# Attention and a gated layer on one core: TensorE's written-out order re-solved, first-block products allowed both single PSUM banks, VectorE named first for two kinds of low parts

## The chip, the cores and the metric

The kernel runs on one core of a Trainium2 chip. The metric is the device time of one execution in microseconds (us). TensorE (PE) multiplies matrices into PSUM banks; VectorE (DVE), ScalarE (ACT) and GpSimd (POOL) work element by element; SyncE (SP) and POOL issue most DMAs. Each engine works its own list of instructions in order and waits on semaphores for the others.

## The reference, cut to what matters

```python
q_bits = (np.einsum('bhsd,dk->bhsk', q, proj) > 0)      # 6 hash bits a row; same for k
mask = q_bucket[:, :, :, None] == k_bucket[:, :, None, :]
scores = np.where(mask, scale * np.matmul(q, k.transpose(0, 1, 3, 2)), -1e9)
attn = softmax(scores)                                   # max taken off, 1e-09 added to the sum
x = (attn @ v).transpose(0, 2, 1, 3).reshape(B * S, H * D)
out = (sigmoid(x @ w_gate) * (x @ w_val)) @ w_out
```

There are 4 batches of 8 heads, 768 rows and a head dimension of 64, so 3072 tokens of width 512; the inner width of the gated layer is 1536. Inputs are float32. To keep their precision, operands are split into a high part in TensorE's float32 format and a low part (what is left), and three products high-low, low-high, high-high are added in PSUM.

## The kernel before, in words

**Attention stage (start to about 405 us).** Sixteen pairs of heads, each in two groups of 384 queries. Per group TensorE does six score tasks (tile `sc`, lines 1551 and 1557: one matmul pair for the hash bits, three for the split products), six transposes (`tp`, L1614) and six value products (`pv`, L1630). A score task fills a double PSUM bank; VectorE takes the minimum and copies it out (`e`, L1569), ScalarE takes the exponential (L1578), TensorE transposes, VectorE or ScalarE copies the transposed block back (`e`, L1620), and TensorE multiplies by the values. There are three double banks, so a score or transpose task waits until the bank of three tasks earlier has been read. Beside that run the preparation of the next pair (transposes `tk` and `tq`, raw copies `rawk` and `rawq`, low parts `kl` and `ql`, a hash product `h`) and the splitting of the gated layer's weights (lines 689 to 712 and 821 to 836), which is spread over VectorE, ScalarE and POOL.

**First block (about 405 to 445 us).** For each of the two groups of batch 0 (a unit) the products of the first two blocks of the inner width are done on their own, `moe_early`: `zg` and `zv` (gate and value, L896), the gated value `gf` (L913), its high and low parts `gh` and `gl` (lines 919 and 920), and the output products `zo` (L932). They wait for the end of the last attention task. A unit first needs its tokens in parts: `load_x` loads `xr`, POOL casts the high part `xh` (L867), and the low part `xl` (L870) may go to POOL or VectorE. Each of these products has one of the two single PSUM banks (tag `one`).

**Remaining products (to the end).** All other blocks go through a seven-product scheme for 2 by 2 blocks (`zB`, `zA`, `zD`, L1178) and output products `y` (L932), with weights streamed in by POOL's DMAs (`wsg`, `wsv`, L1728).

**What sets the order.** Every piece of work is a task with a key and one or more engines that may do it. TensorE follows the list `ORDER`, word for word. For the other engines a planner plays the tasks through with costs written in the code, takes at each free engine the ready task with the smallest key (key plus `SHIFT`, a number for each task), and so fixes each engine's list when the program is built. A task with several engines named stands in the queue of each of them, with 3 added to its key for each place further back; the planner asks the engines in the order PE, ACT, POOL, DVE, SP. Stock such as `one` (2) and `moe` (1) bounds in the planner how many tasks hold a bank at once; the waits of the running program come from the tiles alone.

Of the kernel before, what the change touches and what calls it, by code (L numbers as in the profile page):

```python
# [507 lines left out]
def lsh_attention_glu_kernel(ctx, tc, q, k, v, proj, w_gate, w_val, w_out, out):  # L508
    nc = tc.nc
# [375 lines left out]

    def product(key, u, n, j, x, prev, last, pace=None):

        z = {"bank": ["moe", "one"]}

        def part(c):  # L890
            if c == 0:
# [885 lines left out]
```

## Time and profile before

| what | value |
|---|---|
| runs of the kernel before | 965.33 us median of 3 (964.59 to 965.78) |
| profiled execution, its own time | 965.6 us |
| span of its trace | 963.8 us |
| granted TensorE clock | 0.999 |
| PE busy | 952.0 us (99%) |
| VectorE, ScalarE, POOL busy | 608.2, 548.2, 274.3 us |

Busy is the time in which an engine has at least one instruction at work. Matmuls are pipelined, so a busy PE may still have short waits inside. The time from the span to the execution's own time (1.8 us) lies outside the trace.

### The profile page before, as it was taken

To read this page: it belongs to the slowest core of one execution; us is meant where nothing else is said; L and a number is where in the kernel's file an instruction comes from. 1 tells how busy PE (TensorE), PEld (TensorE's weight loads), DVE (VectorE), ACT (ScalarE), POOL (GpSimd) and SP (SyncE) were. 2 spreads that over 40 slices of the span, in tenths; PEclk is the share of its full clock that TensorE was granted. 3 is DMA by queue.
4 is the path that set the end of the run, shared out by engine and by line. 5 is a ranking of instruction groups with operands and counts; after the bars stand their busy time and mean duration, and the time that the engine had idled before them with its cause. 6 is when DMAs were issued, how large, how long until landed. Compare 5 with 4: busy or idle time off the path is not lost.

```text
span 963.8 us, 20105 instructions
## 1 busy us (share of the span) xinstructions
PE 952.0 (99%) x8067; PEld 774.8 (80%) x8070; DVE 608.2 (63%) x1173; ACT 548.2 (57%) x993; POOL 274.3 (28%) x325
## 2 busy tenths in 40 slices
PE   9999999999999999999999999999999999999998
PEld 5666665666666567689999999999999999999997
DVE  7999898999899898676656743334633336333332
ACT  5988898898888889554334433324433235333322
POOL 4444655666765665630000000000000000000000
PEclk9999999999999999999999999999999999999999
DMA  7666888888897877489966774444744444644421
GB/s 186 175 194 189 224 252 241 244 249 238 263 268 213 233 228 228 171 315 411 370 237 230 280 262 175 153 153 154 271 170 158 170 177 173 222 154 153 154 78 66
DMA packets 116606, 204.37 MB, mean 212 GB/s; under 512 B 63456, under 2 KB 87968, under 8 KB 110624
## 3 DMA queue, kind: packets, MB, share of 16 engines
q1 hardware_dynamic: 107456, 118.08, 39.9%
q0 software_dynamic: 6688, 84.42, 23.7%
q8 instruction: 63, 1.03, 0.4%
q10 hardware_dynamic: 2368, 0.59, 0.3%
q14 instruction: 31, 0.25, 0.1%
HBM read 147.84 MB, written 43.42 MB: 198 GB/s over the span
## 4 chain that ended last, share of the span: by engine, by line
PE 92%; DVE 4%; DMA 2%; ACT 1%; issue 1%; SPq 0%; ACTq 0%; DVEq 0%
PE y L932 20%; PE pv L1630 12%; PE zBg L1178 10%; PE zBv L1178 10%; PE sc L1557 9%; PE tp L1614 7%; PE zDv L1178 5%; PE zDg L1178 5%; PE sc L1551 4%; PE zAg L1178 2%; PE zAv L1178 2%; PE h L1452 1%; DVE e L1569 1%; PE zg L896 1%; PE zv L896 1%; PE idle L642 1%
## 5 line engine op out<-in xcount | busy, mean ns | idle before, releaser
L1569 DVE TENSOR_SCALAR_CACHE_REDUCE e<-sc 128x768 f32<-128x768 f32 x192 | 177.1, 952 | 20.3 <-PE sc L1557 18.5
L1578 ACT ACTIVATE e<-e,st 128x768 f32<-128x768 f32 x192 | 178.9, 933 | 15.1 <-DVE e L1569 13.2
L932 PE MATMUL y<-wo,gh 128*128 128x512 f32 x480 | 151.0, 396 | 0.0
L1630 PE MATMUL pv<-e,vr 128*64 128x384 f32 x768 | 140.7, 496 | 0.0
L1620 ACT COPY e<-tp 128x768 f32<-128x768 f32 x144 | 112.2, 795 | 27.9 <-PE tp L1614 27.1
L1614 PEld LDWEIGHTS tp<-ident,e 64*128 64x128 f32 x2304 | 87.0, 138 | 45.7 <-issue 13.7
L1178 PE MATMUL zBg<-x,wsg 128*128 128x384 f32 x552 | 111.0, 335 | 0.0
L1178 PE MATMUL zBv<-x,wsv 128*128 128x384 f32 x552 | 110.7, 335 | 0.0
L1178 PEld LDWEIGHTS zBg<-x,wsg 128*128 128x128 f32 x552 | 98.2, 188 | 6.6 <-ACT t1g L1186 0.4
L1178 PEld LDWEIGHTS zBv<-x,wsv 128*128 128x128 f32 x552 | 98.3, 188 | 6.0
L932 PEld LDWEIGHTS y<-wo,gh 128*128 128x128 f32 x480 | 89.9, 187 | 15.2
L1614 PE MATMUL tp<-ident,e 64*128 64x64 f32 x2304 | 99.6, 226 | 1.8 <-DVE e L1569 0.9
L1271 ACT CAST gh<-zt 128x384 fp32r<-128x384 f32 x92 | 47.1, 514 | 95.1 <-DVE zt L1266 75.5
L932 PE MATMUL y<-wo,gl 128*128 128x512 f32 x240 | 93.2, 388 | 0.0
L1557 PE MATMUL sc<-kh,ql 64*128 64x384 f32 x192 | 89.8, 468 | 0.0
L1557 PE MATMUL sc<-kh,qsl 64*128 64x384 f32 x192 | 89.8, 468 | 0.0
L1630 PEld LDWEIGHTS pv<-e,vr 128*64 128x64 f32 x768 | 48.2, 136 | 51.3 <-issue 43.0
L1728 POOL DMA_DIRECT2D wsv<-kzv x23 | 12.2, 532 | 236.9 <-PE zDg L1178 224.6
L1728 POOL DMA_DIRECT2D wsg<-kzg x23 | 12.3, 536 | 227.4 <-PE zDv L1178 206.9
L1250 ACT ACTIVATE sig<-sig 128x384 f32<-128x384 f32 x69 | 36.2, 525 | 61.7 <-DVE sig L1193 61.6
L1274 DVE TENSOR_TENSOR gl<-zt,gh 128x384 fp32r<-128x384 f32 x92 | 51.0, 554 | 29.2 <-ACT gh L1271 29.2
L1551 PE MATMUL sc<-kq 64*128 64x384 bf16 x384 | 64.8, 328 | 2.3 <-ACT e L1620 1.1
(214 smaller groups left out, 1964.4 us busy)
## 6 DMA issues: line engine op xcount, KB each, us to landing
wsg<-kzg POOLq DMA_DIRECT2D x23, 1792.0 KB, 8.1
wsv<-kzv POOLq DMA_DIRECT2D x23, 1792.0 KB, 7.6
kzg<-wkg SPq DMA_DIRECT2D x12, 896.0 KB
kzv<-wkv SPq DMA_DIRECT2D x12, 896.0 KB
rawg<-in_moe_w_gate_dram SPq DMA_DIRECT2D x14, 512.0 KB
rawv<-in_moe_w_val_dram SPq DMA_DIRECT2D x14, 512.0 KB
vr<-in_v_dram SPq DMA_DIRECT2D x16, 384.0 KB
rb<-rd SPq DMA_DIRECT2D x64, 96.0 KB
```

Source lines behind the costliest of these rows:

```text
L932: nc.tensor.matmul(acc, a[:, slot, ts_], w, start=(first and i == 0), stop=(last and i == 2), skip_group_check=cols != slice(None),)
L1178: nc.tensor.matmul(acc, streams[n, jp][:, c, wa, a_], X[x_][:, xa, c], start=first and c == 0 and i == 0, stop=c == 1 and i == 2, skip_gro ...
L1250: lambda blk=blk: nc.scalar.activation(sig[:, blk], w["B"][:, :GN] if blk == 2 else sig[:, blk], AF.Sigmoid),
L1271: nc.scalar.copy(side["h"][:, blk], w["z", blk])
L1274: eng.tensor_sub(side["l"][:, blk], w["z", blk], f(side["h"][:, blk]))
L1551: nc.tensor.matmul(sc[:, j, :GN], kq[z["h"]][rows, 2 + 2 * g + h, t * P : (t + 1) * P], kq[z["h"]][rows, h], start=True, stop=False, tile_ ...
L1557: nc.tensor.matmul(sc[:, j, :GN], q_[rows, c], z["k" + x][rows, h * GN : (h + 1) * GN], start=False, stop=(m == 2), tile_position=(j * D, 0),)
L1569: nc.vector.tensor_scalar(sp(e), gz["sc", t, h][:, :, :GN], -MASKED * SCALE, None, op0=ALU.min, op1=ALU.min, accum_out=gz["st", t][:, h : ...
L1578: nc.scalar.activation(e, e, AF.Exp, bias=st[:, h : h + 1], scale=-1.0, accum_out=gz["su"][:, h * GT + t : h * GT + t + 1],)
L1614: nc.tensor.transpose(tp[:, r, at_ : at_ + D], gz["e", t, h][rows, c * P : (c + 1) * P], ident[rows, rows], tile_position=(r * D, 0),)
L1620: copy(gz["e"][:, :, c * P : (c + 1) * P].rearrange("p n (r d) -> p r n d", r=2), gz["tp", c][:, :, :GN].rearrange("p r (n d) -> p r n d", ...
L1630: nc.tensor.matmul(gz["pv"][rows, :GN], z["v"][:, h, c], gz["e"][:, h * GT : (h + 1) * GT, c * P : (c + 1) * P], start=(c == 0), stop=(c = ...
```

## The change

Three things. The stock `moe` is no longer taken by the first-block products whose key is at least 1e4, which is all of them here; they take only `one`. For the low parts `xl` and `gl` VectorE is now named first and POOL second. And `ORDER` and `SHIFT` are new throughout the attention stage and the first block. No computation is added or taken away.

```diff
@@ load_x
-                [("pool", 965, lambda c=c: low(c, nc.gpsimd)), ("dve", 470, lambda c=c: low(c, nc.vector))],
+                [("dve", 470, lambda c=c: low(c, nc.vector)), ("pool", 965, lambda c=c: low(c, nc.gpsimd))],
@@ product
-        z = {"bank": ["moe", "one"]}
+        z = {"bank": ["one"] if key >= 1e4 else ["moe", "one"]}
@@ gated
-            FIRST, [("pool", 965, lambda: low(nc.gpsimd)), ("dve", 470, lambda: low(nc.vector))],
+            FIRST, [("dve", 470, lambda: low(nc.vector)), ("pool", 965, lambda: low(nc.gpsimd))],
@@ moe_early
-        bank = ["y"] if ended else ["moe", "one"]
+        bank = ["y"] if ended else ["one"] if key >= 1e4 else ["moe", "one"]
@@ ORDER (first line of the attention stage that differs)
-    3, 4, 5, 6, 7, 8, 9, 10, 11, 12, 13, 14, 15, 39, 16, 17, 18, 42, 19, 20, 48, 21, 45, 51, 22, 23, 24, 25, 26, 53,
+    3, 4, 5, 6, 7, 8, 9, 10, 11, 12, 13, 14, 15, 39, 16, 17, 18, 42, 19, 20, 48, 21, 22, 45, 51, 23, 24, 25, 26, 27,
```

Three places of the engines' lists. In the names the first number is a buffer, the last one a running number; lines of the changed kernel are 22 higher.

The first is VectorE's list about a quarter of the way through the attention stage, where the tokens of the first unit (`xr_0`) are split. Before:

```order
L1569 TENSOR_SCALAR e_0_1_2237,st_0_1_2_2391<-sc_0_1_2_1_2382 128x768
L870 TENSOR_TENSOR xl_0_2409<-xr_0_2267,xh_0_2408 128x384
L707 SCALAR_TENSOR_TENSOR exv_0_2374<-rawv_0_2239,exv_0_2374 128x512
L870 TENSOR_TENSOR xl_0_2409<-xr_0_2267,xh_0_2408 128x384
L1637 TENSOR_TENSOR xs_3_1_2484<-pv_3_1_2255,rb_3_1_2151 128x384
L870 TENSOR_TENSOR xl_0_2409<-xr_0_2267,xh_0_2408 128x384
L1569 TENSOR_SCALAR e_1_0_2505,st_1_0_0_2504<-sc_1_0_0_0_2475 128x768
```

and with the change:

```order
L1591 TENSOR_SCALAR e_0_1_2277,st_0_1_2_2396<-sc_0_1_2_1_2387 128x768
L892 TENSOR_TENSOR xl_0_2413<-xr_0_2306,xh_0_2412 128x384
L724 SCALAR_TENSOR_TENSOR mfg_0_2383<-rawg_0_2235,mfg_0_2383 128x512
L1591 TENSOR_SCALAR e_1_0_2475,st_1_0_0_2474<-sc_1_0_0_0_2443 128x768
L1642 COPY e_0_0_2019<-tp_0_0_3_2456 128x2x6x64
```

Of the four low parts of this unit VectorE had three and now has one; POOL has the other three. The low parts `gl` stand on the same engines as before (three on POOL, one on VectorE).

The second is TensorE's list at the end of the attention stage. Before:

```order
L1614 MATMUL tp_3_1_0_7420<-ident,e_3_1_7245 128x64 x12
L1614 MATMUL tp_3_0_4_7436<-ident,e_3_0_7048 128x64 x12
L1630 MATMUL pv_3_0_7373<-e_3_0_7048,vr_3_7001 64x384 x2
L1614 MATMUL tp_3_1_1_7455<-ident,e_3_1_7245 128x64 x12
L1614 MATMUL tp_3_1_2_7468<-ident,e_3_1_7245 128x64 x12
L1614 MATMUL tp_3_1_3_7482<-ident,e_3_1_7245 128x64 x12
L1630 MATMUL pv_3_0_7373<-e_3_0_7048,vr_3_7001 64x384 x2
```

and with the change:

```order
L1636 MATMUL tp_3_1_0_7430<-ident,e_3_1_7209 128x64 x12
L1636 MATMUL tp_3_1_1_7444<-ident,e_3_1_7209 128x64 x12
L1636 MATMUL tp_3_1_2_7462<-ident,e_3_1_7209 128x64 x12
L1636 MATMUL tp_3_1_3_7479<-ident,e_3_1_7209 128x64 x12
L1636 MATMUL tp_3_0_5_7497<-ident,e_3_0_7028 128x64 x12
L1636 MATMUL tp_3_1_4_7510<-ident,e_3_1_7209 128x64 x12
L1636 MATMUL tp_3_1_5_7525<-ident,e_3_1_7209 128x64 x12
L1652 MATMUL pv_2_1_7227<-e_2_1_6853,vr_2_6631 64x384 x2
```

Seven transposes now stand in a row, where at most three stood together between value products.

The third is TensorE's list in the first block, from the first output product on. Before:

```order
L932 MATMUL zo_0_0_7662<-wo_1361,gl 128x512
L932 MATMUL zo_0_0_7662<-wo_1361,gh 128x512 x2
L932 MATMUL zo_0_0_7662<-wo_1554,gl 128x512
L932 MATMUL zo_0_0_7662<-wo_1554,gh 128x512 x2
L932 MATMUL zo_0_0_7679<-wo_1361,gl 128x512
L932 MATMUL zo_0_0_7679<-wo_1361,gh 128x512 x2
```

and with the change:

```order
L954 MATMUL zo_0_0_7662<-wo_1391,gl 128x512
L954 MATMUL zo_0_0_7662<-wo_1391,gh 128x512 x2
L954 MATMUL zo_0_0_7662<-wo_1590,gl 128x512
L954 MATMUL zo_0_0_7662<-wo_1590,gh 128x512 x2
L918 MATMUL zg_0_1_7676<-xh_1_7659,we 128x384
L918 MATMUL zg_0_1_7676<-xl_1_7660,we 128x384
```

The second unit's gate product now begins behind the first output product instead of behind the second; the first output product's two halves (`wo_1361` and `wo_1554`, now `wo_1391` and `wo_1590`) stand as close together as before.

## Rows read from the trace of the kernel before

**Rows 1.** The page: span, and busy time of each engine.

```profile
span 963.8 us, 20105 instructions
PE 952.0 (99%) x8067; PEld 774.8 (80%) x8070; DVE 608.2 (63%) x1173; ACT 548.2 (57%) x993; POOL 274.3 (28%) x325
```

**Rows 2.** Busy us by stretch: length, PE, PEld, DVE, ACT, POOL, clock, DMA.

```profile
30.00:405.30 375.30, 370.49 (x4880) 243.16 (x4880) 335.74 (x671) 323.47 (x569) 228.71 (x247) 1.00 0.77 227
...
430.00:963.80 533.80, 529.97 (x2775) 492.56 (x2773) 232.20 (x420) 194.83 (x374) 23.85 (x44) 1.00 0.54 200
```

**Rows 3.** Timeline at the first unit's tokens: start us, duration us, [idle before].

```profile
127.63 1.28 POOL L712 TENSOR_TENSOR mfv<-mfv,exv 128x512 f32<-128x512 f32 x1
...
127.84 1.48 DVE L870 TENSOR_TENSOR xl<-xr,xh 128x384 fp32r<-128x384 f32 x1
...
129.25 0.95 DVE L1569 TENSOR_SCALAR_CACHE_REDUCE e<-sc 128x768 f32<-128x768 f32 x1
...
130.26 0.59 PE L1614 MATMUL tp<-ident,e 64*128 64x64 f32 x12 [0.93 <-DVE e L1569]
```

**Rows 4.** Timeline at 107 us, and durations (min/median/max ns) of line 697.

```profile
107.31 2.09 DVE L697 TENSOR_SCALAR mfg<-rawg 128x512 int32<-128x512 int32 x1
...
107.29 1.83 POOL L1389 TENSOR_TENSOR ql<-rawq,qh 128x768 fp32r<-128x768 f32 x1
...
L697 DVE TENSOR_SCALAR mfg<-rawg x14: 387/420/2092, 28.4 to 476.0; 128x512 int32<-128x512 int32 x14
```

**Rows 5.** Timeline of the start.

```profile
11.63 1.08 DVE L1443 TENSOR_SCALAR kq<-hq,thr_q,mul_q 128x768 bf16<-128x768 f32 x1 [0.19 <-PE hq L1437]
11.74 1.03 PE L642 MATMUL idle<-sig 128*128 128x512 bf16 x4 [0.16 <-issue]
```

**Rows 6.** Timeline of PE at the end of the attention stage.

```profile
394.18 0.87 PE L1630 MATMUL pv<-e,vr 128*64 128x384 f32 x4
394.98 0.96 PE L1614 MATMUL tp<-ident,e 64*128 64x64 f32 x24
...
400.67 1.34 PE L1614 MATMUL tp<-ident,e 64*128 64x64 f32 x36
401.94 3.45 PE L1630 MATMUL pv<-e,vr 128*64 128x384 f32 x20
405.32 0.44 PE L896 MATMUL zg<-xh,we 128*128 128x384 f32 x1
```

**Rows 7.** Groups of the attention stage: xcount, busy us, mean ns, idle before.

```profile
L1620 ACT COPY e<-tp 128x768 f32<-128x768 f32 x144 | 112.2, 795 | 27.9 <-PE tp L1614 27.1
...
L1620 DVE COPY e<-tp 128x768 f32<-128x768 f32 x48 | 45.3, 951 | 5.2 <-PE tp L1614 5.1
...
L1378 DVE TENSOR_SCALAR rawq<-tq 128x768 f32<-128x768 f32 x8 | 7.6, 956 | 2.4 <-PE tq L1358 2.3
...
L1389 DVE TENSOR_TENSOR kl<-rawk,kh 128x768 fp32r<-128x768 f32 x3 | 3.5, 1172 | 0.6 <-ACT kh L1385 0.6
L870 DVE TENSOR_TENSOR xl<-xr,xh 128x384 fp32r<-128x384 f32 x3 | 3.2, 1072 | 0.0
```

**Rows 8.** Timeline of the first block.

```profile
409.59 0.33 PE L896 MATMUL zv<-xh,we 128*128 128x384 f32 x1
...
414.18 0.50 PE L932 MATMUL zo<-wo,gl 128*128 128x512 f32 x1 [0.27 <-POOL gl L920]
...
416.13 0.50 PE L932 MATMUL zo<-wo,gl 128*128 128x512 f32 x1 [0.98 <-DVE gl L920]
...
419.02 0.83 ACT L1035 CAST x<-B 128x768 fp32r<-128x768 f32 x1
```

**Rows 9.** First streamed weights: POOL's issue, issue to landing, first use.

```profile
418.89 0.64 POOL L1728 DMA_DIRECT2D wsg<-kzg  x1
...
wsg<-kzg POOLq DMA_DIRECT2D x23, 1792.0 KB, 8.1
...
428.75 1.22 PE L1178 MATMUL zBg<-x,wsg 128*128 128x384 f32 x6
```

548 rows, old and new, of tables (ORDER, SHIFT) are left out of this document.

## The prediction

> **What bounds the kernel now.** I read the page first. PE is busy for 952.0 of 963.8 us [rows 1], so about 12 us is all that PE ever stands idle; the change neither adds nor removes a matmul. VectorE, the next busiest, has 608.2 us. Whatever the new order does, it can give back only waits of PE or add new ones.
>
> The view by stretches says where those waits are. From 430 us to the end PE works 529.97 of 533.8 us, and what is missing there is the tail behind the last product [rows 2]. The lists of that stretch are the same for PE in both kernels, so I take nothing from it. In the attention stage, from 30 to 405.3 us, PE works 370.49 of 375.3 us: 4.8 us of plain idle time [rows 2]. VectorE works 335.74 us there and has 39.6 us free; ScalarE works 323.47. So PE sets the pace there too, but VectorE, at 89%, is close behind, and when one of its instructions is late PE feels it.
>
> The timeline shows one such place. Where the first unit's tokens are split, VectorE's third low part `xl` takes 1.48 us, beside a POOL instruction that began just before it; the minimum behind it starts at 129.25, and the transpose on PE that needs that minimum's bank has been idle for 0.93 us when it starts at 130.26 [rows 3]. The reader is to see the chain: a filler piece on VectorE, then the minimum, then the bank, then PE.
>
> The first block is short but has waits of its own: the first output product waits 0.27 us for a low part on POOL and its second half 0.98 us for one on VectorE [rows 8]. Together 1.25 us.
>
> **The change part by part.**
>
> *The bank edit itself costs and gives nothing at run time.* The stock `moe` exists in the planner alone. In the trace the value product's matmuls already run without idle time at 409.59, straight behind the gate product, in the other single bank [rows 8]: both banks alternate in the kernel before. What the edit does is to let the planner place work where it believed it had to wait. Value 0.
>
> *VectorE named first.* The planner asks POOL before VectorE whenever both are free, so the order of the names changes little, and the lists go the other way: of the first unit's four low parts VectorE has one instead of three, of the second unit's one instead of two; the `gl` are unmoved. That removes two `xl` of 1.072 us from VectorE in the attention stage [rows 7]. The third one before was the one in front of the late minimum, and no `xl` stands there now. I count the whole 0.93 us as gone; the bounds are 0 (another filler is late in its place) and -0.93.
>
> *VectorE's other work.* Comparing its lists for the attention stage, it gains four copies of transposed blocks at 0.951 (+3.8), one low part at 1.172 (+1.2), loses two raw copies net at 0.956 (-1.9) and the two `xl` (-2.1) [rows 7]: about +0.9 us. It also gains one more set of weight sums with its low part, for which no row of this stage has a price; by the size of the neighbours perhaps 2 us. What hides it is VectorE's 39.6 us of free time [rows 2]. I take 0; without that cover it is up to +3.
>
> *Switches on PE.* A run of one value chunk takes 394.98 - 394.18 = 0.80 us up to the next kind, a run of five takes 405.32 - 401.94 = 3.38 [rows 6]. So each further chunk costs (3.38 - 0.80)/4 = 0.645, and beginning a run costs 0.80 - 0.645 = 0.155. The new list has 73 runs of value chunks instead of 75: -0.3 us. Runs of scores fall from 108 to 105; no pair of rows here isolates that, and by the same price it would be another -0.5, so the bounds are -0.3 and -0.8 and I take -0.5.
>
> *The start.* One more filler matmul (`idle`) now stands ahead of the transpose of the swapped queries, and so ahead of the hash product `hq` on which VectorE waits with an idle time of 0.19 us [rows 5]. Four fillers take 1.03 us, so one takes 0.26; VectorE has nothing else there, and the first scores wait for it. +0.26, from 0 (if the transpose's input is late anyway) to +0.26.
>
> *Seven transposes in a row at the end of the attention stage.* Three in a row took (401.94 - 400.67)/3 = 0.42 us each [rows 6] and found three free banks. The fourth to seventh need the copies of the first four. A copy takes 0.795 us on ScalarE and 0.951 on VectorE [rows 7], so the two engines together empty a bank every 0.433 us, if nothing stands between. The first two copies are both on ScalarE: the first begins about 0.1 us behind its transpose, at 0.52, ends at 1.32, the second ends at 2.11. PE would reach the fourth transpose at 1.27 and the fifth at 1.69, so it loses about 0.1 and then some 0.4. I take +0.5; bounds 0 (copies start earlier) and +1.0 (one VectorE instruction of about 1 us in front of a copy).
>
> *The first block.* The first output product's second half still follows the first at once, and `gl` is still on the same engines, so the 1.25 us stays. The rearranged rows reuse single banks sooner: a gate product's bank is given free by ScalarE, which has casts of 0.83 us [rows 8] in front of that. PE has other products to do meanwhile. I take +0.1; bounds 0 and +0.83.
>
> POOL gets one more `xl` of the second unit in front of its two weight DMAs. Before, the DMA was issued at 418.89, and with the page's median of 8.1 us to landing it is there at 427.0; first use is at 428.75 [rows 9]. That is 1.75 us of cover, and one low part of about 1.1 us [rows 7] fits in it. I take 0; if the cover is gone each us later is a us of time.
>
> *All other short waits of the attention stage.* Its order is new throughout, so the rest of the 4.8 us is dealt again. Nothing that I can read from the lists says to which side: I take 0, and for the range from -4 (nearly all gone) to +4 (doubled).
>
> Sum: -0.93 - 0.5 + 0.26 + 0.5 + 0.1 = -0.6 us. Against the profiled execution, 965.6 us, that is 965.0; the median of the runs is 0.3 us lower, 965.33, so I predict 964.7 us. A measurement of this kernel can tell about 0.2%, 1.9 us, from no change.
>
> **A rule that bears on it.** The row at 107 us shows VectorE's line 697, which has a median of 420 ns, taking 2.09 us beside a POOL instruction that began 0.02 us earlier and ran for 1.83 us [rows 4]. The Trainium skill, "SBUF — State Buffer", section "SBUF: two separate sides", states that VectorE and GpSimd share one port pair as an exclusive lock, held for a whole instruction, so the loser waits in full. The trace agrees. By that rule a low part moved to POOL relieves VectorE less than its own length, and the 0.93 us above could be lost again: the sum by the row is 964.7 us, by the rule, with that term at nothing, 965.6.
>
> **The rivals.**
>
> *The order is better by more than the list shows.* If the re-solved lists clear most of the attention stage's idle time, PE gains up to 4.8 us [rows 2], and short waits inside busy stretches beside it. For: waits like the one at 130.26 are single events that a new order need not repeat. Against: VectorE gets no less work, and as many places as before take a bank whose reader has only just finished. With 3.4 us less than the forecast: 961.3 us.
>
> *VectorE held behind POOL, so slower.* Place: the attention stage, where POOL now has two more `xl` and VectorE more fillers. Price: a held instruction loses 2.09 - 0.42 = 1.67 us [rows 4], and the minimums behind it pass it to PE, as at 130.26. With the forecast's -0.6 a single hold more gives +1.1, still within 0.2%; from two on it is slower: +2.7, or 968.0 us. For: rows 3 and 4 both show such holds. Against: only a part of a hold reached PE in rows 3, and holds that the old order has may go.
>
> *The first weights come late.* If POOL's DMAs are issued more than 1.75 us later, PE waits at the first `zBg`; with 2.5 us it is 0.75 us more, 965.4. Against: one low part is 1.1 us.
>
> *The change does nothing.* The bank edit and the naming are without effect at run time, and if the new order has the same waits elsewhere the time stays at 965.3 us.
>
> **How the numbers follow.** The forecast, 964.7 us with an own range of 962.8 to 966.4: 0.43. Better order, 961.3: 0.27. Held VectorE, 968.0: 0.22. Late weights: 0.03. Nothing: 0.05. The range reaches from 961.0 into the middle of the better-order case to 968.0 into that of the held one; about 0.1 lies beyond each end. Faster by over 0.2% (below 963.4): the better-order case and the lower part of the forecast, 0.27 + 0.11 = 0.38. Slower (above 967.3): 0.22 and a little, 0.23. Within: 0.39.
>
> **What would show it.** The profile after should have PE as busy as before from 430 us on; `zo` waiting about 0.3 and 1.0 us in the first block; no PE wait at the first unit's `xl`; gaps of some 0.5 us in the run of seven transposes; first scores about 0.3 us later. The first `zg` at about 404.7 us instead of 405.32 would confirm the sum. The prediction is wrong if that start moves by over 2 us either way, which is then the idle time of the attention stage, or if PE waits at the first `zBg`.

## The result, and the profile after

The changed kernel takes 970.16 us, median of 4 runs (968.76 to 970.54), beside 964.96 us (963.84 to 965.78) for the kernel before in the same place: ratio 1.0052, 95% interval 1.0035 to 1.0069. It is slower by 5.2 us, and outside the predicted range. Ratios here are not the quotient of the two medians and can differ from it by up to 0.001.

The page, to be read beside [rows 1]:

```profile
span 968.5 us, 20110 instructions
PE 952.4 (98%) x8067; PEld 775.7 (80%) x8070; DVE 607.4 (63%) x1179; ACT 544.9 (56%) x991; POOL 270.4 (28%) x321
```

No engine has more to do (PE's 0.4 us apart). What grew is idle time of PE. Busy us by stretch, as in [rows 2], first the attention stage up to the first `zg`, then the remaining products, 4.8 us later than in [rows 2] because everything is later by that:

```profile
30.00:408.40 378.40, 370.51 (x4869) 243.72 (x4866) 335.19 (x677) 320.54 (x568) 223.44 (x240) 1.00 0.76 226
434.80:968.50 533.70, 529.48 (x2775) 492.61 (x2773) 232.61 (x420) 193.53 (x372) 22.72 (x43) 1.00 0.54 200
```

In the attention stage PE is idle for 378.40 - 370.51 = 7.89 us, where it was 4.81. From the first `zBg` to the end it takes 535.0 us in this kernel and 535.1 in the one before. So the loss lies ahead of that. The waits of PE in the attention stage, summed by what ended them (us in total, times, longest):

```profile
PE sc L1573 <- DVE e L1591: 2.6, 4, 1.3
PE tp L1636 <- DVE e L1591: 1.7, 3, 1.2
PE sc L1573 <- DMA kq<-bd: 1.7, 2, 1.3
...
```

and in the kernel before:

```profile
...
PE h L1452 <- DVE xs L1637: 1.1, 1, 1.1
PE tp L1614 <- DVE e L1569: 0.9, 1, 0.9
...
```

More than half of it is PE waiting for a bank that VectorE's minimum (L1591) empties late: 2.6 and 1.7 us, where the kernel before has 0.9. The timeline shows why. Two of these places, each with what stood in front of the minimum on VectorE and what POOL did beside it:

```profile
301.92 2.31 DVE L729 SCALAR_TENSOR_TENSOR exo<-rawo,exo 128x512 int32<-128x512 int32 x1
301.54 2.15 POOL L1411 TENSOR_TENSOR kl<-rawk,kh 128x768 fp32r<-128x768 f32 x1
305.16 0.34 PE L1573 MATMUL sc<-kq 64*128 64x384 bf16 x2 [0.95 <-DVE e L1591]
...
353.07 2.42 DVE L1411 TENSOR_TENSOR ql<-rawq,qh 128x768 fp32r<-128x768 f32 x1
352.56 2.11 POOL L855 TENSOR_TENSOR wkv<-mfv,wkv 128x896 fp32r<-128x896 f32 x1
356.42 0.59 PE L1636 MATMUL tp<-ident,e 64*128 64x64 f32 x12 [1.23 <-DVE e L1591]
```

An `exo` of L729 takes 0.68 us elsewhere (median) and a low part of this size 0.95 at the shortest. The POOL instructions that began just before them end at 301.54 + 2.15 = 303.69 and 352.56 + 2.11 = 354.67. `exo` and `ql` end 0.54 and 0.82 us behind that, a little less than their own usual length, as if each did its work only when POOL's had ended; the run pool_later below tests this. I call such an instruction held. PE pays about 1 us for each. This is the pattern of [rows 4].

Long holds are not new, and they have not become more. In the attention stage of the kernel before, four VectorE instructions of 0.42 us took 2.06 to 2.09 us beside POOL, at 107, 159, 227 and 325 us; in the changed kernel only `exo` and `ql` are over 2 us. Here is the one at 159 us, in front of the `xs` that PE's product `h` waits for at 162 us:

```profile
159.42 2.07 DVE L697 TENSOR_SCALAR mfv<-rawv 128x512 int32<-128x512 int32 x1
159.39 1.82 POOL L1389 TENSOR_TENSOR ql<-rawq,qh 128x768 fp32r<-128x768 f32 x1
```

Behind the one at 227 us PE shows no wait. What counts is the place: whether TensorE needs the bank behind the held instruction at once (the run swaps below tests this).

The place of [rows 3] has not gone:

```profile
126.18 0.96 POOL L889 CAST xh<-xr 128x384 fp32r<-128x384 f32 x2 [7.40 <-DMA xr<-xd]
126.42 0.39 PE L1573 MATMUL sc<-kq 64*128 64x384 bf16 x2 [1.32 <-DMA kq<-bd]
127.17 1.34 DVE L892 TENSOR_TENSOR xl<-xr,xh 128x384 fp32r<-128x384 f32 x1 [2.92 <-POOL xh L889]
129.35 0.94 DVE L1591 TENSOR_SCALAR_CACHE_REDUCE e<-sc 128x768 f32<-128x768 f32 x1
130.35 0.34 PE L1573 MATMUL sc<-kq 64*128 64x384 bf16 x2 [1.33 <-DVE e L1591]
```

One `xl` stands there instead of three, but VectorE sits idle for 2.92 us in front of it, because POOL's cast waits for the load of the tokens. The minimum behind it is as late as it was. The size of this wait is no fixed property of an order, either: with the attention lists of the kernel before, the transpose there is late by 1.10 us in its own trace, by 0.45 in that of the run edits and by 1.84 in that of newblock (stalls, as taken below). From the load's issue to the first cast it is 7.7, 7.1 and 8.8 us in these three.

The end of the attention stage, beside [rows 6]:

```profile
398.80 1.02 PE L1636 MATMUL tp<-ident,e 64*128 64x64 f32 x26 [0.32 <-ACT e L1600]
399.17 2.98 ACT L1642 COPY e<-tp 128x768 f32<-128x768 f32 x4 [0.43 <-PE tp L1636]
400.02 1.29 PE L1636 MATMUL tp<-ident,e 64*128 64x64 f32 x24 [0.20 <-ACT e L1642]
401.57 0.97 PE L1636 MATMUL tp<-ident,e 64*128 64x64 f32 x24 [0.26 <-DVE e L1642]
402.47 6.03 PE L1652 MATMUL pv<-e,vr 128*64 128x384 f32 x36
```

The seven transposes run from 397.95 to 402.47, 4.52 us where seven at 0.42 are 2.94: 1.58 us lost, the first part for the last exponential, the rest for copies, four of which are in one piece on ScalarE.

The first block, beside [rows 8]: two waits that the old order did not have, and the first weights.

```profile
427.79 0.45 PE L918 MATMUL zv<-xh,we 128*128 128x384 f32 x1 [0.56 <-ACT sig L975]
432.74 0.50 PE L954 MATMUL zo<-wo,gl 128*128 128x512 f32 x1 [0.51 <-POOL gl L942]
433.55 0.69 PE L1200 MATMUL zBg<-x,wsg 128*128 128x384 f32 x3
```

From the first `zg` (408.43) to the first `zBg` it takes 25.13 us; before it was 428.75 - 405.32 = 23.43.

To add waits up finely I also took, for each task of PE, the distance from its start to the next one's, less the 30th percentile that the trace of before shows for the same pair of kinds (score, transpose, value chunk and so on); I call the rest a stall. The percentiles alone sum to 397.98 us in the old order and 397.41 in the new one, 0.57 less. The stalls sum to 23.4 and 29.2 us, with these sums in the stretches spoken of below:

| stretch, us | before | after |
|---|---|---|
| 108 to 135 | 3.13 | 4.42 |
| 162 to 189 | 1.73 | 0.58 |
| 297 to 324 | 1.63 | 2.39 |
| 351 to 378 | 1.18 | 2.87 |
| 378 to 405 | 0.78 | 2.91 |
| 405 to `zBg` | 1.92 | 3.51 |

### The profile page after: what moved, and what is told of

The parts are those of the page before. It is cut to its first block, busy times and chain, and to the rows that moved or that the text cites. A ratio compares the mean times of both kernels' runs of the same rounds, so it can differ in the third digit from the quotient of the medians.

```text
span 968.5 us, 20110 instructions
## 1 busy us (share of the span) xinstructions
PE 952.4 (98%) x8067; PEld 775.7 (80%) x8070; DVE 607.4 (63%) x1179; ACT 544.9 (56%) x991; POOL 270.4 (28%) x321
## 4 chain that ended last, share of the span: by engine, by line
PE 90%; DVE 4%; ACT 2%; DMA 2%; POOL 1%; SPq 1%; issue 1%; DVEq 0%; ACTq 0%; POOLq 0%
PE y L954 20%; PE pv L1652 12%; PE zBg L1200 10%; PE zBv L1200 10%; PE sc L1579 9%; PE tp L1636 7%; PE zDg L1200 5%; PE zDv L1200 5%; PE sc L1573 4%; PE zAv L1200 2%; PE zAg L1200 2%; DVE e L1591 1%; PE h L1474 1%; DMA xr<-xd 1%; ACT e L1600 1%
## 5 line engine op out<-in xcount | busy, mean ns | idle before, releaser
L1591 DVE TENSOR_SCALAR_CACHE_REDUCE e<-sc 128x768 f32<-128x768 f32 x192 | 176.9, 952 | 17.4 <-PE sc L1579 15.0
L1642 ACT COPY e<-tp 128x768 f32<-128x768 f32 x140 | 109.1, 794 | 29.5 <-PE tp L1636 28.7
```

The costliest lines, as they stand in the source:

```text
L1591: nc.vector.tensor_scalar(sp(e), gz["sc", t, h][:, :, :GN], -MASKED * SCALE, None, op0=ALU.min, op1=ALU.min, accum_out=gz["st", t][:, h : ...
L1642: copy(gz["e"][:, :, c * P : (c + 1) * P].rearrange("p n (r d) -> p r n d", r=2), gz["tp", c][:, :, :GN].rearrange("p r (n d) -> p r n d", ...
```

## The experiments

Twelve kernels were run. The table gives what each measured. The kernel before was run beside them, the changed kernel was not, so its 970.2 us and its trace are from the first measurement. The kernel before has 964.28 us in the first four, 964.42 in the next four and 964.34 in the last four.

| kernel | us, median | ratio to before, 95% |
|---|---|---|
| edits | 965.8 | 1.0017 (1.0009 to 1.0026) |
| oldblock | 966.69 | 1.0025 (1.0014 to 1.0036) |
| newblock | 965.65 | 1.0015 (1.0007 to 1.0024) |
| oldend | 977.59 | 1.0132 (1.0117 to 1.0147) |
| late_tokens | 972.45 | 1.0080 (1.0068 to 1.0092) |
| swaps | 966.32 | 1.0021 (1.0012 to 1.0030) |
| endfill | 968.44 | 1.0040 (1.0027 to 1.0053) |
| all_fixed | 969.35 | 1.0049 (1.0037 to 1.0061) |
| endold | 967.53 | 1.0033 (1.0019 to 1.0047) |
| fixed2 | 965.24 | 1.0005 (0.9991 to 1.0019) |
| best | 965.16 | 0.9999 (0.9983 to 1.0016) |
| pool_later | 967.25 | 1.0026 (1.0012 to 1.0040) |

**The edits without the new order (edits).** The code of the change with both old tables.

```diff
-ORDER, SHIFT  # of the changed kernel
+ORDER, SHIFT  # of the kernel before
```

> The changed code with the old ORDER and SHIFT, so the stock and naming edits alone. Lists of the attention stage stay those of before; in the first block a few VectorE and ScalarE pieces change places. Theory 1 (the edits only let the planner choose; the loss is in the new order): 965.0 us, within 1 us of before, first zg at 405.3. Rival (the naming or the bank edit itself puts work in a worse place): at least 1.5 us slower than before, 966.5 or more, with new waits of PE between 414 and 430 us.

No engine's list in the attention stage moves, and the first block keeps 23.42 us. The kernel is 0.17% slower all the same, some 1.6 us. In the trace PE has one new wait, behind the first `zBg`:

```profile
429.62 1.34 PE L1178 MATMUL zBg<-x,wsg 128*128 128x384 f32 x6 [0.99 <-ACT t1g L1186]
```

A cast of `B` stands three places later on ScalarE's list, waits 2.09 us for VectorE there, and the copy `t1g` behind it is late. So with the old numbers the edits alone cost some 1.3 us (from the first `zBg` to the end 536.4 us instead of 535.1). That is nearer to the rival than to theory 1: a piece of work in a worse place, and a loss of 1.6 us (0.9 to 2.5) where the rival had at least 1.5 and theory 1 at most 1. The wait ends at 429.62 us, at the very end of the stretch that the rival named, though behind the first `zBg` and not in front of it. Which of the edits moves the cast no run shows. The changed kernel's own numbers don't have this wait.

**Attention and first block apart (oldblock, newblock).** In the changed kernel the old order of the first block (2059 to 2068 are output products `zo` of the first unit, 2080 to 2093 gate and value products of the second), with the old `SHIFT` of these tasks (cut here: one more output product, 2109, and the numbers of `SHIFT`); newblock is the mirror, old attention with the new first block.

```diff
-    2038, 2040, 2041, 2042, 2043, 2045, 2046, 2047, 2048, 2052, 2053, 2054, 2055, 2059, 2060, 2080, 2081, 2063,
-    2064, 2082, 2083, 2085, 2086, 2067, 2087, 2088, 2068, 2090, 2091, 2092, 2093, 2097, 2098, 2099, 2100, 2104,
+    2038, 2040, 2041, 2042, 2043, 2045, 2046, 2047, 2048, 2052, 2053, 2054, 2055, 2059, 2060, 2063, 2064, 2080,
+    2081, 2082, 2083, 2085, 2086, 2087, 2088, 2090, 2091, 2092, 2093, 2067, 2068, 2097, 2098, 2099, 2100, 2104,
...
```

> The changed kernel with the old order of the first block (ORDER and SHIFT from task 2035 on are those of before), attention as changed. Theory 1 (the loss is spread over places that are independent of each other; from the first zg to the first zB the changed kernel takes 25.13 us instead of 23.43): 1.7 us less than the changed kernel's 970.2, so 968.5; first zg still at 408.4, first zB 23.4 behind it. Rival (the first block is slow because ScalarE and POOL come out of the new attention stage with work left over): no gain, 970.2.

> The changed code with the old attention order and the new first block: the mirror. Theory 1: 1.7 us more than before, 966.7; first zg at 405.3, PE waits of 0.7 us at a zv behind ScalarE's tanh and of 0.6 us at a zo behind a low part on POOL. Rival (the block's waits come from work left over by the new attention stage): as before, 965.0, without these two waits.

The first block takes 23.54 us in oldblock and 25.12 in newblock, whatever attention order stands ahead of it. The waits of PE in the first block of newblock:

```profile
PE zo L954 <- DVE gl L942: 1.0, 1, 1.0
PE zo L954 <- POOL gl L942: 0.8, 2, 0.5
PE zv L918 <- ACT sig L975: 0.4, 1, 0.4
```

Oldblock has only the first line and 0.3 us of the second. So the new block costs 1.6 to 1.7 us with either attention order; the rival falls. It is not TensorE's order alone: in the run endold below, TensorE has the same order, ScalarE has one cast fewer in front of its second tanh, PE has no wait at `zv`, and the block takes 24.32 us. Oldblock came out lower than 968.5 because in its trace the attention stage, from the first score on, was 3.1 us shorter than the changed kernel's, with the same lists; 3.0 us of that lie between 108 and 135 us (1.46 us of stalls instead of 4.42).

**The old end, first try (oldend).** From about 380 us on the old `ORDER` and `SHIFT`, first block included.

```diff
-ORDER[585:], SHIFT of what starts later  # of the changed kernel
+ORDER[585:], SHIFT of what starts later  # of the kernel before
```

> The changed order up to about 380 us, from there the old order of TensorE and the old SHIFT, first block included. The run of seven transposes is gone. Theory 1: the run cost 1.6 us in waits, with others near it about 1.9, so 1.9 us less than with the old first block alone: 970.2 - 1.7 - 1.9 = 966.6; first zg at 406.5. Rival (the transposes are late because copies are scarce in this stretch whatever the order, so the waits go to other tasks): 968.5, first zg at 408.4.

The stalls from 378 to 405 us fall from 2.91 to 1.04, as theory 1 has it, and from the last score task to the first `zg` it takes 14.26 us, as before, instead of 15.27. But the first weights come late; as I read POOL's list, pieces of weight splitting that the two orders do at different times collide there:

```profile
430.31 1.06 POOL L920 TENSOR_TENSOR gl<-gf,gh 128x384 fp32r<-128x384 f32 x1 [8.58 <-ACT gh L919]
431.31 0.64 POOL L1728 DMA_DIRECT2D wsg<-kzg  x1
439.29 1.94 PE L1178 MATMUL zBg<-x,wsg 128*128 128x384 f32 x5 [6.15 <-ACT x L1035]
```

POOL issues them at 431.31 instead of 418.89 [rows 9], ScalarE's operands are late too, and PE stands for 6.15 us. The granted clock, too, stood at its lower level (1.2 GHz; 0.50 and 0.51 of full speed) from 418.7 to 422.1 us and from 435.7 to 442.6. It fell the first time within a wait of PE of 1.78 us, the second time within the one of 6.15, and from the first `zBg` to the end this trace takes 537.2 us instead of 535.0. The total says nothing on the end of the attention stage, then.

**The tokens (late_tokens).** From here on a short list moves single tasks of the finished lists and leaves everything else as it is: in each pair the first task is put right behind the second.

```diff
+        for m, a in MOVE:
+            x = next(o for o in out if o[5] == m)
+            out.remove(x)
+            out.insert(next(i for i, o in enumerate(out) if o[5] == a) + 1, x)
```

Here the eight casts and low parts of the first unit go behind a minimum of the next group, and the second unit's load behind them.

```diff
+MOVE = [(2027, 575), (2029, 2027), (2028, 2029), (2030, 2028), (2031, 2030), (2032, 2031), (2033, 2032), (2034, 2033), (2071, 2034)]
```

> The changed kernel; only the casts and low parts of the first unit's tokens (and the load behind them) stand some 10 us later in the lists, behind the minimum of the next group. Theory 1 (the load of the tokens, issued at about 116 us, lands anywhere from 122.6 to 126.2 in the five traces so far; POOL and then VectorE stand in order behind it, and PE lost 1.54 and 1.55 us at 126.42 and 130.35 to that): 1 to 3 us less than the changed kernel's 970.2, so 967.2 to 969.2, no idle time of VectorE before xl and less spread between runs. Rival (all transfers are late there, the hash bits too): the wait for the bits of 1.3 us stays, and at most 1.5 us is gained.

It became slower than the changed kernel: 1.0080. The wait for the hash bits at 126 us stays (1.6 us), as the rival said. The wait for the minimum at 130 is gone, but the low parts now stand beside other work of VectorE, some 7 us later (first cast at 133.30 instead of 126.18):

```profile
135.77 1.31 POOL L898 TENSOR_TENSOR xl<-xr,xh 128x384 fp32r<-128x384 f32 x1
136.13 1.76 DVE L1417 TENSOR_TENSOR ql<-rawq,qh 128x768 fp32r<-128x768 f32 x1
138.83 0.59 PE L1642 MATMUL tp<-ident,e 64*128 64x64 f32 x12 [1.05 <-DVE e L1597]
140.30 2.09 POOL L861 TENSOR_TENSOR wkg<-mfg,wkg 128x896 fp32r<-128x896 f32 x1
141.04 1.65 DVE L717 TENSOR_SCALAR exv<-rawv 128x512 int32<-128x512 int32 x1
145.16 0.59 PE L1642 MATMUL tp<-ident,e 64*128 64x64 f32 x12 [1.40 <-ACT e L1648]
```

Again VectorE is long beside POOL (`ql` 1.76, and an `exv` of L717 1.65 where 0.42 is usual), and PE pays at the next minimum, or through ScalarE, which waits for `exv` with its copies queued behind. My theory of this place falls in its main part: moving the tokens only moved the collision.

**VectorE's order at the two holds (swaps).** `exo` and `ql` behind the next minimum.

```diff
+MOVE = [(1913, 1283), (1577, 1487)]
```

> The changed kernel with two pairs on VectorE exchanged: the exponent piece exo at 302 us and the low part ql at 353 us stand behind the next minimum instead of in front of it. Theory 1 (these two were held to 2.31 and 2.42 us beside POOL instructions of 2.1 us, and the minimums behind them cost PE 1.17 and 1.38): 2.2 us less than the changed kernel's 970.2, so 968.0; the stalls at 305 and 356 go below 0.4. Rival (VectorE is over-full there, and a held piece passes its loss to whatever stands behind it): the stalls move to the next transposes or scores, 970.2.

1.0021, where the changed kernel had 1.0052. The stall at 305 is gone, the one at 356 is down to 0.37, together some 2 us. The stretch of the tokens, which this edit doesn't touch, is shorter in this trace too (2.05 us of stalls from 108 to 135 instead of 4.42). In this trace `ql` is still held:

```profile
349.70 1.91 DVE L1417 TENSOR_TENSOR ql<-rawq,qh 128x768 fp32r<-128x768 f32 x1
```

but the minimum that PE needs is done before it. For these two stalls theory 1 holds.

**POOL's instruction elsewhere (pool_later).** VectorE's list as changed; only POOL's `kl` goes behind its next piece.

```diff
+MOVE = [(1369, 1914)]
```

> The changed kernel with VectorE's list as it is and one POOL instruction elsewhere: the low part kl that began at 301.54 us stands behind POOL's next piece, so it no longer runs beside VectorE's exo. Theory 1 (VectorE was held for POOL's instruction): exo takes 0.7 us instead of 2.31, the stall of 1.17 at 305 goes, 1.1 us less than the changed kernel. Rival (exo was long for another reason, such as traffic of the transfers): exo stays above 1.5 us and the stall stays.

```profile
299.55 0.68 DVE L735 SCALAR_TENSOR_TENSOR exo<-rawo,exo 128x512 int32<-128x512 int32 x1
...
301.62 1.86 POOL L1417 TENSOR_TENSOR kl<-rawk,kh 128x768 fp32r<-128x768 f32 x1
```

`exo` takes 0.68 us instead of 2.31, and PE no longer waits at that score task. That it was POOL's instruction that held it is shown by this; for `ql` no run moves POOL's instruction, and that it was held the same way is read from the timeline. The second stall, at 353 us here, is still there (1.62). The total fell by more than the 1.1 us expected, as this trace too has less between 108 and 135 us (1.60).

**The end (endfill, endold).** Endfill moves three value chunks in between the seven transposes:

```diff
+MOVE = [(1565, 1650), (1624, 1654), (1625, 1619)]
```

> The changed kernel with three value chunks moved from behind the seven transposes to between them, TensorE's list alone. Theory 1 (the four waits of 0.54, 0.32, 0.28 and 0.43 are filled, less three more switches at 0.155): 1.1 us less than the changed kernel's 970.2, so 969.1; first zg 1.1 us earlier. Rival (the copies' rate is the limit and the last value products wait for the last copies anyway): 970.2.

Endold gives TensorE the old alternation behind the last score task (1642) and lets the planner place the rest:

```diff
-1642, 1558, 1564, 1621, 1616, 1622, 1623, 1650, 1652, 1654, 1656, 1618, 1658, 1660, 1565, 1624, 1625, 1662,
-1663, 1664, 1665, 1666, 1667
+1642, 1558, 1564, 1621, 1565, 1650, 1616, 1622, 1652, 1654, 1656, 1623, 1662, 1663, 1664, 1618, 1658, 1660,
+1665, 1624, 1625, 1666, 1667
```

> The changed kernel; behind the last score task TensorE's list alternates transposes and value chunks as before, and the other engines follow by the planner's rules. Theory 1 (what made the end slow is that the nine value chunks were left for last, so that seven transposes in a row met only four copies on ScalarE in one piece): waits between 378 and 405 us fall from 2.9 to about 1 us, first zg 1.5 us earlier than in the changed kernel, counted from the last score task 13.8 us instead of 15.3. Rival, from the run with three chunks between (the exponentials and copies behind the last score are the limit): the 15.3 us stay, the waits go to other tasks.

Both theories of the run of seven fall. In endfill 378 to 405 us has 2.83 us of stalls, and from the last score to the first `zg` it takes 15.86 us; in endold 14.98 (and 2.37 us of stalls), against 15.27 in the changed kernel and 14.26 before. That endold's total is lower all the same (1.0033) comes with its first block, 24.32 us instead of 25.13, as said. One row of endfill and one of endold:

```profile
400.78 0.87 PE L1658 MATMUL pv<-e,vr 128*64 128x384 f32 x4 [0.84 <-ACT e L1648]
...
395.89 0.65 PE L1636 MATMUL tp<-ident,e 64*128 64x64 f32 x14 [0.93 <-ACT e L1600]
```

The wait goes to a copy in the one and to the last exponential in the other. What stands ahead of the last score has to do with it: starts of the last score tasks on PE, of before and then of after.

```profile
384.21 0.36 PE L1551 MATMUL sc<-kq 64*128 64x384 bf16 x2
384.91 0.36 PE L1551 MATMUL sc<-kq 64*128 64x384 bf16 x2
389.94 0.33 PE L1551 MATMUL sc<-kq 64*128 64x384 bf16 x2
391.06 0.34 PE L1551 MATMUL sc<-kq 64*128 64x384 bf16 x2
```

```profile
390.37 0.33 PE L1573 MATMUL sc<-kq 64*128 64x384 bf16 x2
391.06 0.34 PE L1573 MATMUL sc<-kq 64*128 64x384 bf16 x2
391.76 0.34 PE L1573 MATMUL sc<-kq 64*128 64x384 bf16 x2
393.16 0.34 PE L1573 MATMUL sc<-kq 64*128 64x384 bf16 x2 [0.17 <-DVE e L1591]
```

Before, two and two, 5 us apart; after, four together. So four minimums of 0.95 and their exponentials queue up just ahead of the end. That this is the cause is argued from these rows and from oldend, which has the old places and 14.26 us; no run has it alone.

**Putting it together (all_fixed, fixed2, best).** All_fixed: old first block, tokens late, swaps and endfill. Fixed2: old first block and swaps. Best: fixed2 with endold.

```diff
+MOVE = [(1913, 1283), (1577, 1487)]  # fixed2, best; on the tables of oldblock
```

> The changed attention order with the three edits above and the old first block. Theory 1 (five places that add up): 970.2 - 1.7 - 2.0 - 2.2 - 1.1 = 963.2, 1 us under the kernel before (964.3 in the last runs). Rival (the places share their slack: what one stall gives back, the next wait takes): 966 or more, the old first block's 966.7 at most improved by 1.

> The changed attention with the two exchanges on VectorE and the old first block; the tokens where the change has them. Theory 1 (exchanges and block add up): old block alone was 1.0025 of before, the two exchanges gave 2.2 us at 305 and 356; together 964.5, level with before. Rival (gains overlap): 966.5.

> As the one before, with the end of the attention stage as before too. Theory 1: 1.5 us less again, 963.0, a little under the kernel before. Rival (the end's length is set behind the last score): 964.5, level with before.

All_fixed pays for the late tokens (6.05 us of stalls from 135 to 162 us). About 1.6 us of that lie where the clock was low: behind two waits of PE for minimums (1.50 us at 137.5, 1.94 at 145.2) the granted clock is 0.53 of full speed from 146.0 to 149.6 us, nearly all of it at the lower level (1.2 GHz). Fixed2 is level with the kernel before, as theory 1 has it: old block and two exchanges take back the loss. Best is level too, without the 1.5 us more that its theory 1 expected; no version here beats the kernel before.

## Why the prediction was wrong, point by point

How large the loss is, the runs say in two ways: 5.2 us directly (3.4 to 6.7), and some 4 us by the kernels that share most of its lists, if each took away just what its trace shows: oldblock's 1.0025 and its 1.6 us (0.0017) make 1.0042; pool_later's 1.0026 and 1.1 us make 1.0037; swaps' 1.0021 and 2.2 us make 1.0044.

**"All other short waits of the attention stage. I take 0."** This is the step that failed outright: a term put at nothing because the lists could not tell it. What stood in its place are above all the holds at 302 and 353 us: stalls of 1.17 and 1.38, shown by pool_later and swaps. That is the mechanism of the rival "VectorE held behind POOL", to which I gave 0.22. Its price for VectorE was right: two holds, 1.63 us longer (`exo`) and 1.47 (`ql`) beside the 1.67 that I had, and only a part of each arriving at PE. Its reason was not: neither hold is beside an `xl`, and long holds became fewer, two instead of four; these two stand where PE needs the bank at once. And it doesn't make the total: the old order's own waits, 1.15 at a hash product at 162 us, itself behind a hold, and 0.78 at a transpose at 331, did go.

So this term came out at about +1.3 (the stretches of the two holds below, +2.45, less the 1.15 that went). Of the 5.8 us between the forecast of -0.6 and the measured +5.2 that is less than a quarter; the end of the attention stage (+2.1 where I had +0.5), the first block (+1.7 where I had +0.1) and the `xl` (0 where I had -0.93) are the other three, each mis-sized in the same direction.

**Seven transposes, +0.5 (0 to +1.0).** Mechanism right, size wrong: 1.58 us for the run itself. I priced the copies from the first transpose on, and left out that VectorE would be busy (weight sums to 400.33, its first copy at 400.60), so that four copies stood in a row on ScalarE, and that the second group's exponential would be late. Endfill and endold show that filling the run doesn't give it back.

**The first block, +0.1 (0 to +0.83).** Mis-sized: +1.6 to +1.7, shown by oldblock and newblock. My two `zo` waits were right (1.0 and 0.3 us, still there). What I took for work that PE would do meanwhile was not enough: `zv` waits for a tanh behind casts on ScalarE, as I had it for a gate product's bank, and the last `zo` for a low part on POOL. The two new waits are 1.07 us; the rest is in shorter stalls.

**The `xl`, -0.93.** Not gained. The row of [rows 3] was read as filler work that is late. It is the load of the tokens that is late, and POOL and VectorE stand in order behind it, with three low parts or with one. With the lists of before the delay was anything from 0.45 to 1.84 us in three traces, so a term of 0.93 from one of them could not be counted on. That I also named the sum with this term at nothing (965.6 us) is luck: I had a held `xl` in mind there, and it was the load.

**Switches, -0.5.** The sum over pairs of kinds gives -0.57. **The start, +0.26.** The first score starts at 13.37 us instead of 13.70; over the kernels with the new start it lies between 12.88 and 14.11, over those with the old between 13.23 and 13.87, so a quarter of a microsecond can't be seen there.

**Bank edit, 0.** The lists of the attention stage and the waits of the first block are the same in edits and before, as said. The 1.3 us that edits loses further on comes from ScalarE's order. The first weights were not late in the changed kernel, and the part behind the first `zBg` takes as long as before, as predicted, though PE's list there is not quite the same: one output product (2109) stands five places earlier.

**The sign.** A first `zg` later by over 2 us was to show that the loss is in the attention stage. It came 3.1 us later (408.43), and the loss there is real, but the sign is weak: with the same attention lists it stands at 405.32 us before, 405.03 in newblock and 402.95 in edits.

By these sums the loss is made of: first block +1.7, the holds' stretches +2.45 (0.76 and 1.69), the end +2.1, the wait that went -1.15 (162 to 189 us), switches -0.57: +4.5 us, and differences elsewhere of under 1 us a stretch, of both signs, besides the +1.3 of 108 to 135 us. Between 108 and 135 us the order decides nothing that the runs can tell (last section).

## What to carry to other kernels

In a kernel whose first engine is busy 99% of the time, a new order of everything redistributes waits, and "zero" for what can't be read from lists is a bet: look for pairs of long POOL and VectorE instructions that would stand side by side in front of an instruction that frees a bank which TensorE needs next, and count each as about a microsecond lost (1.15, 1.17 and 1.38 us here). Where TensorE has other work until then a hold costs nothing that the trace shows, as at 227 us before. A held instruction is cheap behind the minimum that TensorE needs and dear in front of it, so exchange it there. Don't move filler work out of one tight place without looking what it then stands beside: with the tokens moved by some 7 us the ratio was 1.0080 instead of 1.0052.

## What the runs showed of the hardware

The load of the first unit's tokens (768 KB) lands at very different times with the same lists. Issue and first cast in oldblock, and then in best, whose lists are the same up to there:

```profile
116.83 0.41 SPq L859 DMA_DIRECT2D xr<-xd  x1
123.81 0.96 POOL L866 CAST xh<-xr 128x384 fp32r<-128x384 f32 x2 [4.26 <-DMA xr<-xd]
```

```profile
116.85 0.40 SPq L865 DMA_DIRECT2D xr<-xd  x1
126.29 0.96 POOL L872 CAST xh<-xr 128x384 fp32r<-128x384 f32 x2 [7.35 <-DMA xr<-xd]
```

From issue to the cast it is 7.0 us in the one and 9.4 in the other; 7.1 to 8.8 in three traces of the old order and 7.0 to 9.4 in nine of the new. In the new order the four traces with 8.6 us and more have 3.3 to 4.4 us of stalls between 108 and 135 us, the five with 7.6 and less have 1.5 to 2.3. So profiles of one and the same order can differ by 2 to 3 us there, and a comparison of two single profiles can't give that place to the change. What makes the landing late I have not settled.

The Trainium skill, "SBUF — State Buffer", section "SBUF: two separate sides", states that the port pair which VectorE and GpSimd share is an exclusive lock, held for a whole instruction. The trace agrees: `exo` took 2.31 us beside `kl` and 0.68 without it.
